# Reordering the tail of a fused hash-attention and mixture-of-adapters kernel: the gates, the sums and tile 5

## The chip, the cores and the metric

The kernel runs on one core of a Trainium2 chip. The metric is the device time of one execution in microseconds. A core has five engines with one instruction queue each: TensorE (PE) for matmuls, VectorE (DVE), ScalarE (ACT), GpSimd (POOL), and SyncE (SP), which here issues most of the transfers. An engine takes its instructions in the order in which the program gives them, so the order in which Python emits work is the order on each engine.

## The reference

Two stages. First an attention over 4 batches, 8 heads, 768 positions and 64 columns, in which a query sees only the keys of its own hash bucket (6 sign bits of a projection). The heads of a position, side by side, give a row x of 512 numbers, 3072 rows in all. Then a mixture of 8 low-rank adapters adds a correction to each row:

```
logits = x @ w_gate                      # 8 numbers a row
topk = the two largest logits            # K = 2
w = exp(sel - max) / sum                 # weights of the two
delta = sum over the two of w * ((x @ A[e]) @ B[e])     # rank 16
out = x + delta
```

## The kernel before, in words

Rows are handled in tiles of 128; a batch has six of them, numbered 0 to 5. The attention runs over 16 pairs of heads (four to a batch); each pair has six slots of scores, whose exponentials ACT takes. The adapter work of a batch is spread over the slots of the next one, except for the last batch, which has nothing behind it: its adapter work is the tail of the kernel, and the change is made there.

The tail is written out by hand, in `lasts` (from slot 2 of the last pair) and in `end`. It splits the six tiles into three groups: H is tiles 0, 1 and 2, I is tiles 3 and 4, J is tile 5. A group goes through these steps:

- `normt` (L360 to L380): DVE divides the attention sums by their denominators; for J it writes a bf16 copy for the transpose, and `xf` (L382) has ACT write the fp32 values of tile 5 into x, in two instructions.
- `turnt` (L390): PE transposes the last 128 columns, ACT or DVE copies them back.
- `lgz` (L402): PE multiplies by the gate weights and all A matrices side by side: 8 logits and 128 numbers z a row, in a PSUM tile lz (lzH, lzI, lzJ).
- the gates. For H, `route1` and `route_exp` leave a mask m and exponentials e; `gates` (L431) then has DVE make gw (L436) and zm = z times gw (L438), and `gsum` (L444) the sum and its reciprocal rt. For I and J, `top` (L453) has DVE find the two largest logits and ACT take the exponentials (L462); `gates1` (L465) then has DVE make gw with its sum (L474), zm and rt. For one tile alone (J) `gates1` multiplies zm by rt at once (L480); for two tiles rt is kept for later (L483, L484).
- `zt` (L493): PE transposes zm (L500), ACT copies the result to zT (L502).
- `product` (L504): PE multiplies zT by all B matrices into a 128x512 PSUM tile d (d0 to d5).
- `total` (L518): out = d times rt plus x. DVE does it in one instruction (L526); with `split`, ACT multiplies (L523) and POOL adds x (L524).
- `store` (L528): one tile of 256 KB goes to the output, from SP's queue or from ACT's.

In the kernel before, `end` orders this so: gates of H follow `normt` of J and `xf`; the sums of tiles 0 (split), 1 (DVE) and 2 (split) follow; then `gates1` of I, `zt` of I, `gates1` of J, `zt` of J, then products 3, 4 and 5. Tile 5 is summed on PE: two fp32 matmuls with the identity (L959) put x of tile 5 into d5, the product is added to it, and ACT copies d5 out (L972). The stores stand in SP's queue in the order of tiles 1, 0, 3, 2, 4; that of tile 5 is on ACT's queue.

Of the kernel before, what the change touches and what calls it, by code (L numbers as in the profile page):

```python
# [12 lines left out]
F32 = mybir.dt.float32  # L13
BF16 = mybir.dt.bfloat16
AX = mybir.AxisListType
ALU = mybir.AluOpType
# [3 lines left out]
class Emitter:  # L20
# [407 lines left out]
        self.nc.scalar.activation(out=e, in_=d, func=ACT.Exp)  # L428
        self.rg[b, I] = (m, e)

    def gates(self, b, I):  # L431
        nc, P, E, r, n = self.nc, self.P, self.E, self.r, len(I)
        lz = self.lz[b, I]
        m, e = self.rg[b, I]
        gw = self.smallp.tile([P, n, E], F32, tag=f"gw{n}", name=f"gw{b}_{I[0]}")
        nc.vector.tensor_mul(out=gw, in0=m, in1=e)  # L436
        zm = self.zm[b, I] = self.smallp.tile([P, n, self.ER], BF16, tag=f"zm{n}", name=f"zm{b}_{I[0]}")
        nc.vector.tensor_tensor(  # L438
            out=zm.rearrange("p n (e r) -> p n e r", e=E),
            in0=lz[:, :, E:].rearrange("p n (e r) -> p n e r", e=E),  # L440
            in1=gw.unsqueeze(3).to_broadcast([P, n, E, r]), op=ALU.mult)
        self.rg[b, I] = gw

    def gsum(self, b, I):  # L444
        nc, P, n = self.nc, self.P, len(I)
# [19 lines left out]
    def gates1(self, b, I):  # L465
        nc, P, E, r, n = self.nc, self.P, self.E, self.r, len(I)
        lz = self.lz[b, I]
        top, e = self.rg[b, I]
        gw = self.smallp.tile([P, n, E], F32, tag=f"gw{n}", name=f"gw{b}_{I[0]}")
        ss = self.smallp.tile([P, n], F32, tag=f"ss{n}", name=f"ss{b}_{I[0]}")  # L470
        zm = self.zm[b, I] = self.smallp.tile([P, n, self.ER], BF16, tag=f"zm{n}", name=f"zm{b}_{I[0]}")
        rt = self.smallp.tile([P, n], F32, tag=f"rt{n}", name=f"rt{b}_{I[0]}")
        for i in range(n):
            nc.vector.scalar_tensor_tensor(out=gw[:, i], in0=lz[:, i, 0:E], scalar=top[:, i, 1:2], in1=e[:, i],  # L474
                                           op0=ALU.is_ge, op1=ALU.mult, accum_out=ss[:, i:i + 1])
        z4, l4 = zm.rearrange("p n (e r) -> p n e r", e=E), lz[:, :, E:].rearrange("p n (e r) -> p n e r", e=E)
        g4 = gw.unsqueeze(3).to_broadcast([P, n, E, r])
        if n == 1:
            nc.vector.reciprocal(out=rt, in_=ss)
            nc.vector.scalar_tensor_tensor(out=z4[:, 0], in0=l4[:, 0], scalar=rt, in1=g4[:, 0],  # L480
                                           op0=ALU.mult, op1=ALU.mult)
            return
        nc.vector.tensor_tensor(out=z4, in0=l4, in1=g4, op=ALU.mult)  # L483
        nc.vector.reciprocal(out=rt, in_=ss)  # L484
        for j, i in enumerate(I):
            self.rt[b, i] = rt[:, j:j + 1]
# [428 lines left out]
    def end(self):  # L915
        nc, P, b, Z = self.nc, self.P, self.B - 1, self.LZ
        H, I, J = (0, 1, 2), (3, 4), (5,)
        self.s_ctx.close()
        pe = self.tc_ctx.enter_context(self.tc.tile_pool(name="ps_e", bufs=1, space=bass.MemoryType.PSUM, reuse_waits="tile"))

        def bank(t):
            return lambda shape, dt, name: pe.tile(shape, dt, tag=t, name=name)

        x0, x1, x2, y0, y1, y2 = (bank(t) for t in ("x0", "x1", "x2", "y0", "y1", "y2"))
        f = [P, 512]
        lz = lambda a, n: a[:, 0:n * Z].rearrange("p (n z) -> p n z", n=n)
        self.pvt(I, 4)
        self.unit(J, x0(f, F32, "pvJ"))
        lzI = lz(x1(f, F32, "lzI"), 2)
        for i in I:  # L930
            self.lgz(b, I, i, range(3), lzI)
        self.normt(I, True)
        self.route_exp(b, H)
        self.pvt(J, 5)
        self.normt(J)
        self.turnt(I, x2, nc.scalar.copy)
        lzJ = lz(y1(f, F32, "lzJ"), 1)
        self.lgz(b, J, 5, range(3), lzJ)
        self.turnt(J, y0, nc.scalar.copy)
        self.xf(J)  # L940
        self.gates(b, H)
        for i in I:
            self.lgz(b, I, i, (3,))
        self.lgz(b, J, 5, (3,))
        self.zt(b, H, y2)
        self.top(b, I)
        self.top(b, J)
        self.gsum(b, H)
        d0, d1, d2 = self.m(f, F32, "d0"), x2(f, F32, "d1"), self.vt(f, F32, "d2")
        self.product(b, 0, d0)  # L950
        self.product(b, 1, d1)
        self.total(b, 0, d0, True)
        self.total(b, 1, d1)
        self.store(b, 0, 1)
        self.store(b, 0, 0)
        self.product(b, 2, d2)
        self.total(b, 2, d2, True)
        d5 = x0(f, F32, "d5")
        nc.tensor.matmul(out=d5, lhsT=self.ident, rhs=self.x[b][:, 5, :], start=True, stop=False,  # L959
                         skip_group_check=True)  # L960
        self.gates1(b, I)
        self.zt(b, I, y2)
        self.gates1(b, J)
        d3, d4 = y0(f, F32, "d3"), x1(f, F32, "d4")
        self.zt(b, J, self.m)
        self.product(b, 3, d3)
        self.product(b, 4, d4)
        self.total(b, 3, d3)
        self.store(b, 1, 1)
        self.store(b, 1, 0)  # L970
        self.product(b, 5, d5, False)
        nc.scalar.copy(out=self.out_to(b, 5), in_=d5)  # L972
        self.total(b, 4, d4)
        self.store(b, 2, 0)
        self.store(b, 2, 1, nc.scalar)


# [46 lines left out]
```

## Time and profile before

| | |
|---|---|
| three runs | 162.53, 163.56, 164.48 us |
| median | 163.56 us |
| the profiled execution, its time | 162.41 us |
| its span, first to last instruction | 160.6 us |
| busy share of the span | PE 93%, ACT 90%, POOL 69%, DVE 68% |
| mean granted TensorE clock | 0.994 |

All times in views of the trace count from the start of the span, which is 1.8 us shorter than the time of its execution. In a timeline row the first number is the start, the second the time from the start of the first to the end of the last of the merged instructions, then engine, line, operation, what is written and read, shapes and count; what stands in brackets is idle time of that engine just ahead and the instruction that ended it. An instruction can start before the one ahead of it on its engine has ended where it does not need its result.

### The profile page before, as it was taken

What the parts mean: (1) busy time and instruction counts of PE and PEld (TensorE: products, weight loads), DVE (VectorE), ACT (ScalarE), POOL (GpSimd) and SP (SyncE); (2) the same over time, 40 slices, a digit from 0 to 9 for tenths busy, and PEclk for the clock granted to TensorE, in tenths of its full rate; (3) what the DMA queues carried; (4) which work ended last, traced back from release to release, by engine and by line L of the source; (5) the groups of instructions that cost most, each with busy time, mean ns of one, the idle gap of its engine ahead of it and who ended that gap; (6) DMA issues with size and microseconds to landing.
All of it is one profiled execution on the core that took longest, in us unless ns stands there. A gap on an engine that the chain in (4) does not pass through costs nothing.

```text
span 160.6 us, 5335 instructions
## 1 busy us (share of the span) xinstructions
PE 148.6 (93%) x2172; PEld 100.8 (63%) x2172; DVE 109.1 (68%) x291; ACT 144.2 (90%) x126; POOL 111.5 (69%) x166
## 2 busy tenths in 40 slices
PE   6898999999999999999998999999999999999730
PEld 2345676676767676667755676667666766788300
DVE  5798895746464976778556976687677527666760
ACT  3798889999999999999997999999999999998830
POOL 7866999998979786969199767988498825320140
PEclk9999999999999999999999999999999999999997
DMA  5996559899998986989979997999788920854054
GB/s 142 291 373 187 172 159 180 230 247 206 260 218 166 267 164 148 232 196 356 169 231 246 291 252 180 253 267 339 162 173 217 230 58 18 234 172 147 2 205 187
DMA packets 57594, 33.03 MB, mean 206 GB/s; under 512 B 42978, under 2 KB 55266, under 8 KB 57570
## 3 DMA queue, kind: packets, MB, share of 16 engines
q1 hardware_dynamic: 57296, 32.43, 80.1%
q8 instruction: 17, 0.28, 0.7%
q10 hardware_dynamic: 274, 0.27, 0.5%
q14 instruction: 7, 0.06, 0.1%
HBM read 20.16 MB, written 7.03 MB: 169 GB/s over the span
## 4 chain that ended last, share of the span: by engine, by line
PE 82%; DVE 8%; DMA 3%; issue 1%; DVEq 1%; ACT 0%; SPq 0%
PE s L283 36%; PE pv L303 19%; PE hs L193 7%; PE pv L291 4%; PE tr L241 4%; DMA nat<-in_k_dram 3%; PE lz L407 3%; PE dl L505 2%; PE warm L646 2%; DVE aug L570 1%; DVE R L180 1%; DVE aug L589 1%; DVE acc L526 1%; DVE x L323 1%; DVEq L1019 1%
## 5 line engine op out<-in xcount | busy, mean ns | idle before, releaser
L286 ACT ACTIVATE P<-s 128x1536 bf16<-128x1536 f32 x96 | 133.9, 1451 | 4.5 <-PE s L283 3.1
L283 PE MATMUL s<-aug 71*128 71x512 bf16 (+2 forms) x432 | 78.5, 308 | 0.9 <-DVE aug L570 0.7
L283 PEld LDWEIGHTS <-aug 71*128 71x128 bf16 x432 | 34.6, 97 | 21.6 <-issue 5.8
L303 PEld LDWEIGHTS <-P 128*128 128x128 bf16 x1080 | 42.1, 98 | 8.2
L303 PE MATMUL pv<-vb,P 128*128 128x65 bf16 x1080 | 44.3, 193 | 0.0
L261 POOL COPY aug<-aug 64x768 bf16<-64x768 bf16 x30 | 24.8, 827 | 14.8 <-DMA aug<-nb 12.3
L180 DVE STREAM_TRANSPOSE R<-nat 128x384 f32<-128x384 f32 x62 | 33.2, 559 | 2.1 <-DMA nat<-in_k_dram 1.9
L232 POOL CAST nb<-nat 128x768 bf16<-128x768 f32 x30 | 24.6, 823 | 2.1 <-DMA nat<-in_k_dram 1.2
L333 POOL CAST xb<-x 128x768 bf16<-128x768 f32 x15 | 12.3, 823 | 12.3 <-DVE x L323 5.8
L526 DVE SCALAR_TENSOR_TENSOR acc<-dl,rt,x 128x512 f32<-128x512 f32 x18 | 13.5, 748 | 7.9 <-PE dl L505 7.9
L323 DVE TENSOR_TENSOR x<-pv,ri 128x384 f32<-128x384 f32 x30 | 16.7, 557 | 1.0
L170 POOL TENSOR_TENSOR vs<-vn 128x384 f32<-128x384 f32 x16 | 15.9, 994 | 0.0
L321 DVE RECIPROCAL ri<-pv 128x6 f32<-128x6 f32 x30 | 5.8, 195 | 14.7 <-PE pv L303 14.6
L247 DVE TENSOR_SCALAR aug<-tr 128x768 bf16<-128x768 bf16 x20 | 11.0, 550 | 5.7 <-PE tr L241 2.3
L193 PE MATMUL hs<-R,hst 128*32 128x192 f32 x240 | 14.0, 332 | 0.0
L168 POOL CAST vb<-vn 128x768 bf16<-128x768 f32 x16 | 13.2, 826 | 0.2 <-DMA vn<-in_v_dram 0.2
L193 PEld LDWEIGHTS hs<-R,hst 128*32 128x32 f32 x240 | 6.7, 109 | 6.3 <-DVE ri L321 4.1
L291 PE MATMUL pv<-vb,eps 128*128 128x390 bf16 x30 | 10.1, 337 | 0.6 <-DVE gw L436 0.3
L241 PE MATMUL tr<-ident_bf,nb 128*128 128x128 bf16 x120 | 10.0, 219 | 0.0
L524 POOL TENSOR_TENSOR acc<-acc,x 128x512 f32<-128x512 f32 x2 | 2.5, 1268 | 9.3 <-ACT acc L523 9.3
L173 POOL TENSOR_TENSOR vb<-vs,vs 128x128 bf16<-128x128 f32 x16 | 7.3, 456 | 1.3
L172 POOL TENSOR_TENSOR vs<-vs 128x128 f32<-128x128 f32 x16 | 7.3, 454 | 1.3
(115 smaller groups left out, 112.3 us busy)
## 6 DMA issues: line engine op xcount, KB each, us to landing
vn<-in_v_dram SPq DMA_DIRECT2D x16, 384.0 KB, 8.1
nat<-in_q_dram SPq DMA_DIRECT2D x15, 384.0 KB
nat<-in_k_dram SPq DMA_DIRECT2D x15, 384.0 KB, 3.9
out_dram<-acc SPq DMA_DIRECT2D x7, 512.0 KB, 4.3
out_dram<-acc SPq DMA_DIRECT2D x9, 256.0 KB, 3.4
dr<-sg SPq DMA_DIRECT2D x14, 48.0 KB, 2.5
aug<-dr SPq DMA_DIRECT2D x14, 48.0 KB
nat<-in_q_dram SPq DMA_DIRECT2D x2, 192.0 KB
```

Of the source, the lines that this page charges most:

```text
L170: nc.gpsimd.tensor_add(out=s3, in0=vn[:, :, 0:3, :], in1=vn[:, :, 3:6, :])
L180: self.nc.vector.transpose(out=self.R[p][:, i, h, :], in_=self.nat[p][:, i, h, :])
L193: nc.tensor.matmul(out=hs[32 * j:32 * j + 32], lhsT=self.hst[:, hf].rearrange("p b i -> p (b i)"), rhs=rhs, start=(hf == 0), stop=(hf == 1 ...
L232: self.nc.gpsimd.tensor_copy(out=self.nb[p][:, i].rearrange("p t h d -> p h t d"), in_=self.nat[p][:, i].rearrange("p h (t d) -> p h t d", ...
L241: self.nc.tensor.transpose(out=tr[:, t, :], in_=self.nb[p][:, i, t].rearrange("p h d -> p (h d)"), identity=self.ident_bf)
L261: self.nc.gpsimd.tensor_copy(out=a[0:64, :, 2 + i, :], in_=a[64:128, :, i, :])
L283: nc.tensor.matmul(out=ps[:, o:o + w].rearrange("p (t c) -> p t c", c=P), lhsT=aug[0:71, kt, 2 * h + 1, :], rhs=rhs, start=True, stop=True)
L286: nc.scalar.activation(out=self.P_[p][:, s * W:end], in_=ps, func=ACT.Exp, scale=128.0)
L291: self.nc.tensor.matmul(out=pv, lhsT=self.eps, rhs=self.vb[p % 3][:, h, T:T + 1, :].to_broadcast([self.P, T, D + 1]), start=True, stop=Fal ...
L303: self.nc.tensor.matmul(out=pv[:, i, :], lhsT=self.P_[p][:, o:o + P], rhs=vb[:, h, kt, :], start=False, stop=(kt == T - 1), skip_group_che ...
L323: nc.vector.tensor_tensor(out=self.x[b][:, :, c:c + D], in0=pv[:, :, 0:D], in1=ri.unsqueeze(2).to_broadcast([P, T, D]), op=ALU.mult)
L526: nc.vector.scalar_tensor_tensor(out=out, in0=ps, scalar=rt, in1=self.x[b][:, i, :], op0=ALU.mult, op1=ALU.add)
```

## The change

The gates of H are split: `gates` makes gw ahead of `normt` of J, and the new `gated` makes zm right after it. `xf` moves from behind `turnt` of J to a place behind the sums of tiles 0 to 2. `zt` of H moves ahead of the last `lgz` step of J. `gates1` of I moves ahead of the sum of tile 1, and `zt` of I ahead of the split sum of tile 2. Product 2 moves ahead of the sum of tile 0. Products 3 and 4 move ahead of `zt` of J. The identity matmuls and ACT's copy of tile 5 go; DVE sums tile 5 with `total`, and for that `gates1` no longer has a form of its own for one tile. The order of the stores in the queues stays as it was.

```diff
--- before.py
+++ after.py
@@ -428,18 +428,24 @@
         self.nc.scalar.activation(out=e, in_=d, func=ACT.Exp)
         self.rg[b, I] = (m, e)
 
-    def gates(self, b, I):
+    def gates(self, b, I, then=True):
         nc, P, E, r, n = self.nc, self.P, self.E, self.r, len(I)
         lz = self.lz[b, I]
         m, e = self.rg[b, I]
         gw = self.smallp.tile([P, n, E], F32, tag=f"gw{n}", name=f"gw{b}_{I[0]}")
         nc.vector.tensor_mul(out=gw, in0=m, in1=e)
+        self.rg[b, I] = gw
+        if then:
+            self.gated(b, I)
+
+    def gated(self, b, I):
+        nc, P, E, r, n = self.nc, self.P, self.E, self.r, len(I)
+        lz, gw = self.lz[b, I], self.rg[b, I]
         zm = self.zm[b, I] = self.smallp.tile([P, n, self.ER], BF16, tag=f"zm{n}", name=f"zm{b}_{I[0]}")
         nc.vector.tensor_tensor(
             out=zm.rearrange("p n (e r) -> p n e r", e=E),
             in0=lz[:, :, E:].rearrange("p n (e r) -> p n e r", e=E),
             in1=gw.unsqueeze(3).to_broadcast([P, n, E, r]), op=ALU.mult)
-        self.rg[b, I] = gw
 
     def gsum(self, b, I):
         nc, P, n = self.nc, self.P, len(I)
@@ -475,11 +481,6 @@
                                            op0=ALU.is_ge, op1=ALU.mult, accum_out=ss[:, i:i + 1])
         z4, l4 = zm.rearrange("p n (e r) -> p n e r", e=E), lz[:, :, E:].rearrange("p n (e r) -> p n e r", e=E)
         g4 = gw.unsqueeze(3).to_broadcast([P, n, E, r])
-        if n == 1:
-            nc.vector.reciprocal(out=rt, in_=ss)
-            nc.vector.scalar_tensor_tensor(out=z4[:, 0], in0=l4[:, 0], scalar=rt, in1=g4[:, 0],
-                                           op0=ALU.mult, op1=ALU.mult)
-            return
         nc.vector.tensor_tensor(out=z4, in0=l4, in1=g4, op=ALU.mult)
         nc.vector.reciprocal(out=rt, in_=ss)
         for j, i in enumerate(I):
@@ -931,47 +932,45 @@
             self.lgz(b, I, i, range(3), lzI)
         self.normt(I, True)
         self.route_exp(b, H)
+        self.gates(b, H, False)
         self.pvt(J, 5)
         self.normt(J)
+        self.gated(b, H)
         self.turnt(I, x2, nc.scalar.copy)
         lzJ = lz(y1(f, F32, "lzJ"), 1)
         self.lgz(b, J, 5, range(3), lzJ)
         self.turnt(J, y0, nc.scalar.copy)
-        self.xf(J)
-        self.gates(b, H)
         for i in I:
             self.lgz(b, I, i, (3,))
+        self.zt(b, H, y2)
         self.lgz(b, J, 5, (3,))
-        self.zt(b, H, y2)
         self.top(b, I)
         self.top(b, J)
         self.gsum(b, H)
         d0, d1, d2 = self.m(f, F32, "d0"), x2(f, F32, "d1"), self.vt(f, F32, "d2")
         self.product(b, 0, d0)
         self.product(b, 1, d1)
+        self.product(b, 2, d2)
         self.total(b, 0, d0, True)
+        self.gates1(b, I)
         self.total(b, 1, d1)
         self.store(b, 0, 1)
         self.store(b, 0, 0)
-        self.product(b, 2, d2)
+        self.zt(b, I, y2)
         self.total(b, 2, d2, True)
-        d5 = x0(f, F32, "d5")
-        nc.tensor.matmul(out=d5, lhsT=self.ident, rhs=self.x[b][:, 5, :], start=True, stop=False,
-                         skip_group_check=True)
-        self.gates1(b, I)
-        self.zt(b, I, y2)
+        self.xf(J)
         self.gates1(b, J)
-        d3, d4 = y0(f, F32, "d3"), x1(f, F32, "d4")
-        self.zt(b, J, self.m)
+        d3, d4, d5 = y0(f, F32, "d3"), x1(f, F32, "d4"), x0(f, F32, "d5")
         self.product(b, 3, d3)
         self.product(b, 4, d4)
+        self.zt(b, J, self.m)
         self.total(b, 3, d3)
         self.store(b, 1, 1)
         self.store(b, 1, 0)
-        self.product(b, 5, d5, False)
-        nc.scalar.copy(out=self.out_to(b, 5), in_=d5)
+        self.product(b, 5, d5)
         self.total(b, 4, d4)
         self.store(b, 2, 0)
+        self.total(b, 5, d5)
         self.store(b, 2, 1, nc.scalar)
 
 
```

## The prediction

> **What bounds the kernel now.** I read the page's head first, then the chain of work that ended last, then the timeline of each engine from 147 us on, and last the transfers in short windows. Most of the 160.6 us lies ahead of the change and is the same program in both kernels; only what comes after 148.5 us can move.
>
> ```profile
> span 160.6 us, 5335 instructions
> ```
>
> The chain of work, cut to the tail, says who sets the order there:
>
> ```profile
> 151.39 0.75 DVE acc L526
> 152.14 0.30 DVE gw L474 x4
> ...
> 154.44 1.18 DVEq L1019
> ```
>
> DVE's sum of tile 1 (L526) is followed by the gates of tiles 3 and 4 on the same engine: these waited for the sum, not for their data. The chain then ends at DVE's queue at 155.62, five microseconds before the span does. What fills these five is seen in the stores (SP's rows one by one, ACT's row, SP's waits at the end) and in the DMA share by window (last two columns: share, GB/s):
>
> ```profile
> 152.17 0.33 SPq L535 DMA_DIRECT2D out_dram<-acc  x1
> 153.23 0.33 SPq L535 DMA_DIRECT2D out_dram<-acc  x1
> 154.99 0.33 SPq L535 DMA_DIRECT2D out_dram<-acc  x1
> 155.42 0.38 SPq L535 DMA_DIRECT2D out_dram<-acc  x1
> 155.89 0.41 SPq L535 DMA_DIRECT2D out_dram<-acc  x1
> ...
> 155.36 0.38 ACTq L535 DMA_DIRECT2D out_dram<-acc  x1
> ...
> L1019 SPq EVENT_SEMAPHORE  x7: 17/28/28, 159.1 to 160.6; - x7
> ```
> ```profile
> 153.00:153.75 0.75, 0.25 (x3) 0.08 (x4) 0.60 (x4) 0.37 (x1) 0.75 (x2) 1.00 0.92 350
> ...
> 154.05:154.80 0.75, 0.66 (x3) 0.10 (x1) 0.59 (x1) 0.27 (x2) 0.38 (x1) 1.00 0.91 347
> 154.80:155.75 0.95, 0.00 (x0) 0.00 (x0) 0.82 (x2) 0.53 (x1) 0.00 (x0) 1.00 0.01 2
> 156.00:158.50 2.50, 0.00 (x0) 0.00 (x0) 0.00 (x0) 0.00 (x0) 0.00 (x0) 1.00 1.00 380
> 158.50:158.75 0.25, 0.00 (x0) 0.00 (x0) 0.00 (x0) 0.00 (x0) 0.00 (x0) 0.70 0.37 131
> ```
>
> Six stores of 262144 bytes. A store issued at 152.17 has its first bytes at 153.00, so 0.83 after the issue begins. The first two go alone. Then the DMA engines idle for 0.95, and four stores, issued within 0.9 us, queue at a share of 1.00 until about 158.59 (158.50 plus 0.37 of 0.25). At 380 GB/s one store takes 0.69; at the 350 of a lone one 0.75. So the end is a queue of transfers; the engines set only when each store joins it. From the last byte to the span's end lie 2.0 us of landing and closing that I leave as they are.
>
> **The change part by part.** The rows of the trace before that carry the terms, DVE, then ACT, then PE and POOL:
>
> ```profile
> 148.80 0.29 DVE L372 TENSOR_TENSOR xbt<-pvJ,rit 128x128 bf16<-128x128 f32 x1
> 149.01 0.17 DVE L436 TENSOR_TENSOR gw<-m,e 128x24 f32<-128x24 f32 x1
> 149.22 0.56 DVE L438 TENSOR_TENSOR zm<-lzH,gw 128x384 bf16<-128x384 f32 x1
> 149.73 0.25 DVE L457 MAX8 top<-lzI 128x8 f32<-128x8 f32 x2
> ...
> 150.56 0.18 DVE L449 RECIPROCAL rt<-ss 128x3 f32<-128x3 f32 x1
> 152.06 0.22 DVE L474 SCALAR_TENSOR_TENSOR gw<-lzI,top,e 128x8 f32<-128x8 f32 x1
> 152.46 0.42 DVE L483 TENSOR_TENSOR zm<-lzI,gw 128x256 bf16<-128x256 f32 x1
> 152.80 0.15 DVE L484 RECIPROCAL rt<-ss 128x2 f32<-128x2 f32 x1
> 152.88 0.20 DVE L474 SCALAR_TENSOR_TENSOR gw<-lzJ,top,e 128x8 f32<-128x8 f32 x1
> 153.32 0.35 DVE L480 SCALAR_TENSOR_TENSOR zm<-lzJ,rt,gw 128x128 bf16<-128x128 f32 x1
> 154.21 1.41 DVE L526 SCALAR_TENSOR_TENSOR acc<-d,rt,x 128x512 f32<-128x512 f32 x2 [0.54 <-PE d L505]
> ```
> ```profile
> 149.58 0.52 ACT L388 ACTIVATE x<-pvJ,rit 128x64 f32<-128x64 f32 x2
> 150.21 0.48 ACT L502 COPY zT<-ztp 128x384 bf16<-128x384 bf16 x1
> 150.59 0.43 ACT L462 ACTIVATE e<-lzI,nt 128x8 f32<-128x8 f32 x2
> ...
> 151.17 1.26 ACT L523 ACTIVATE acc<-d,rt 128x512 f32<-128x512 f32 x2
> 153.27 0.37 ACT L502 COPY zT<-ztp 128x256 bf16<-128x256 bf16 x1 [0.83 <-PE ztp L500]
> 154.00 0.27 ACT L502 COPY zT<-ztp 128x128 bf16<-128x128 bf16 x1 [0.36 <-PE ztp L500]
> 154.74 0.58 ACT L972 COPY acc<-d 128x512 f32<-128x512 f32 x1 [0.48 <-PE d L505]
> ```
> ```profile
> 149.84 0.34 PE L500 MATMUL ztp<-ident_bf,zm 128*128 128x128 bf16 x3
> 150.75 0.82 PE L505 MATMUL d<-Bcat,zT 128*128 128x512 bf16 x3 [0.57 <-ACT zT L502]
> 151.40 1.02 PE L959 MATMUL d<-x,ident 128*128 128x512 f32 x2
> 152.94 0.28 PE L500 MATMUL ztp<-ident_bf,zm 128*128 128x128 bf16 x2 [0.52 <-DVE zm L483]
> ...
> 151.94 2.49 POOL L524 TENSOR_TENSOR acc<-acc,x 128x512 f32<-128x512 f32 x2 [9.31 <-ACT acc L523]
> ```
>
> *Split gates of H, `xf` later.* gw of H drops into the time in which DVE waited for PE ahead of tile 5's reciprocal, so it costs nothing there; without that gap it would cost the 0.2 from gw to zm in the rows. zm moves from 149.22 to 149.01, the transposes from 149.84 to 149.63, their copy on ACT from 150.21 to 150.00. `xf` ended at 150.10 and would have held that copy, so its move gives about half of the 0.21. The exponentials of I go from 150.59 to 150.38 and end 0.43 later, at 150.81; the maxima at 149.73 hang on PE's logits and stay, and so does rt of H at 150.56. The last logit step of J now stands behind the transposes on PE, a delay under 0.1 that DVE's two maxima of I cover; what waits for it, J's exponential, has a microsecond to spare.
>
> *Gates of I ahead of the sum of tile 1.* gw starts at 150.85 instead of 152.06; from there by the rows to zm 0.40 and to its end 0.42, so 151.67. The sum of tile 1 takes its place behind the reciprocal, 0.08 after it: 151.67 to 152.42, where it ended at 152.14. This is the price: the first store goes from 152.17 to 152.45.
>
> *`zt` of I and the split sums.* Transposes 0.06 after zm, 151.73 to 152.01; PE is free, because the 1.02 us of identity matmuls are gone. Tile 0's part on ACT goes from 151.17 to 150.97 and ends at 151.65, so the copy to zT (372 ns) runs from 152.05 to 152.42, 1.2 earlier than before. Tile 2's part on ACT now stands behind that copy: 152.33 to 153.01, 0.57 later than before. POOL covers this: its first sum ends at about 153.0, its second runs from 153.1 to 154.36 (it ended at 154.43). Without that cover tile 2's store would come 0.57 later.
>
> *Products 3 and 4, gates of J, `xf`.* Product 3 at 152.48, done at 152.87. On DVE gw of J at 152.34 (two sums in a row start 0.66 apart, from 1.41 less 0.75), zm about 0.25 later (bounds 0.20, half of I's 0.40, and 0.44, from gw to zm in the old form with the reciprocal between), 0.29 long like the 128-wide row at 148.80: 152.87. Sum 3 from 152.91, sum 4 from 153.57, sum 5 from 154.23 to 154.98. Sum 5 needs d5: transpose 152.93 to 153.16, ACT's `xf` ends near 153.45, then the copy (0.27), the product (0.39 and 0.06 of wait): 154.16. That margin is thin, but a delay there moves only the last store. In place of ACT's copy (0.58) DVE does one more sum (0.75), and the old end of sums, 155.62, becomes 154.98.
>
> *The stores*, as issued before and after: tile 1 152.17, 152.45; tile 0 153.23, 153.02; tile 3 154.99, 153.68; tile 2 155.42, 154.39; tile 4 155.89, 154.87 (0.48 behind the issue ahead of it, as now); tile 5, on ACT, 155.36, 155.02. Adding 0.83, they join the queue at 153.28, 153.85, 154.51, 155.22, 155.70 and 155.85. With 0.69 each the DMA engines end them at 153.97, 154.66, 155.35, 156.04, 156.73 and 157.42: none finds the queue empty, and the idle 0.95 of the window rows is gone. 158.59 less 157.42 is 1.17; with 0.75 each the end is 157.78 and the gain 0.81. I take 0.69, since back to back is how they now run, and call it 1.2. The bound on the other side is the last store alone, issued at 155.02: 155.85 plus 0.75 is 156.60, a gain of 2.0.
>
> [...]
>
> Sum: 162.41 less 1.2 is 161.2 for the profiled execution. That execution lies 1.15 under the median of the runs shown, so the forecast for a median is 163.56 less 1.2, 162.4.
>
> **The rivals.** *R1, the queue is faster than thought:* the end is set by the last store alone, gain 2.0, 161.6. For it: the first bytes of lone stores reach 0.9 share at once. Against: 380 GB/s at a share of 1.00 leaves nothing.
>
> [...]
>
> *R4, the change does not do what it says:* the exponentials of I stay late, at 150.59, since ACT is held by something else. Then gates, first store and all else come 0.21 later, a gain near 1.0; that lies inside the forecast's own range.
>
> **How the numbers follow.** The forecast (R4 in it) 0.62, R1 0.13, R2 0.12, R3 0.08, something not seen 0.05. The forecast's own gain is 0.8 to 1.4; the runs shown spread by 1 us about their median, and a median of few runs by about 0.7. 1% is 1.6 us, about what a measurement of this kernel can tell from no change. The forecast reaches over it by spread in 4 of 10 cases (0.25), R1 mostly (0.11): faster 0.36. R3 and the unseen pass 1% on the slow side in 0.06; the rest, 0.58, is within. Range: 161.0, R1 less half a microsecond of spread, to 163.9, R2 with a little; R3 is left out.
>
> **What would show it.** Right: a first store near 152.45 and a third near 153.7; zm of I ending near 151.7 and zm of J near 152.9; three sums in a row on DVE ending near 155.0; no idle DMA window from 153.3 on, and the last bytes near 157.4; a span near 159.4. Wrong: sums of over 0.8 us or POOL sums over 1.3 where they overlap (R2, R3); a last sum that waits for ACT beyond 155.6; gaps in the DMA share between stores; a first store after 153.

## The result, and the profile after

| | before | changed |
|---|---|---|
| median of 20 runs each | 163.72 us | 162.0 us |
| the profiled execution, its span | 162.41, 160.6 us | 162.86, 161.1 us |
| ratio of times | | 0.9918, 95% interval 0.9891 to 0.9945 |

The kernel became faster by 0.82%, 1.34 us (0.9 to 1.8 by the interval). The ratio is of the runs in the faster of two states alone, so it is not that of the two medians, which lie 1.72 us apart. The forecast was 1.2 us less and a median of 162.4.

The profiled execution after has a *longer* span than the one before, so spans cannot be compared as they are. Its last score exponential on ACT, which ends the part that both kernels share, ended later (first row: the kernel before, six of them merged; second row: the changed kernel):

```profile
139.39 8.38 ACT L286 ACTIVATE P<-s 128x1536 bf16<-128x1536 f32 x6 [0.33 <-PE s L283]
```
```profile
span 161.1 us, 5327 instructions
...
147.98 1.45 ACT L286 ACTIVATE P<-s 128x1536 bf16<-128x1536 f32 x1
```

It ended at 147.77 before and at 149.43 after, 1.66 later; nothing ahead of it was changed. From here on, times with a plus count from that end. So counted, the tail to the end of the span took 12.86 before and 11.64 after: 1.2 less. The tail repeats far better than the kernel: the same program profiled a second time gave 11.64 again (e1 and e10 below show the one exception).

The stores of the changed kernel, tiles 1, 0, 3, 2, 4 from SP's queue and tile 5 from ACT's, and the DMA windows (a row has its length, the busy time of PE, of PE's weight loads, of DVE, ACT and POOL, then the granted clock, the DMA share and GB/s; the share reads up to 1.01 here):

```profile
154.07 0.33 SPq L536 DMA_DIRECT2D out_dram<-acc  x1
154.67 0.33 SPq L536 DMA_DIRECT2D out_dram<-acc  x1
155.34 0.33 SPq L536 DMA_DIRECT2D out_dram<-acc  x1
156.03 0.33 SPq L536 DMA_DIRECT2D out_dram<-acc  x1
156.46 0.41 SPq L536 DMA_DIRECT2D out_dram<-acc  x1
...
156.66 0.36 ACTq L536 DMA_DIRECT2D out_dram<-acc  x1
```
```profile
154.07:154.90 0.83, 0.67 (x3) 0.21 (x3) 0.80 (x5) 0.83 (x4) 0.73 (x2) 1.00 0.00 0
154.90:155.00 0.10, 0.00 (x0) 0.00 (x0) 0.10 (x1) 0.10 (x2) 0.10 (x1) 1.00 0.90 348
155.00:159.00 4.00, 0.39 (x1) 0.10 (x1) 1.63 (x3) 0.23 (x2) 1.01 (x1) 0.77 1.01 380
159.00:159.25 0.25, 0.00 (x0) 0.00 (x0) 0.00 (x0) 0.00 (x0) 0.00 (x0) 0.50 0.23 74
```

The two idle stretches of the kernel before are gone. From 154.9, 0.83 after the first issue, the DMA engines run at a share of 1.01 and 380 GB/s for the whole four microseconds, and 1.9 us after the queue runs dry the span ends, as before. Read to 0.01 us from the last packet of the stores, the last byte was written at +10.95 before (158.72) and +9.75 after (159.18). That number is used below; the window rows bracket it.

The engine rows behind the stores, DVE, ACT and POOL of the changed kernel:

```profile
150.66 0.55 DVE L445 TENSOR_TENSOR zm<-lzH,gw 128x384 bf16<-128x384 f32 x1
...
152.48 0.23 DVE L480 SCALAR_TENSOR_TENSOR gw<-lzI,top,e 128x8 f32<-128x8 f32 x1
...
152.90 0.42 DVE L484 TENSOR_TENSOR zm<-lzI,gw 128x256 bf16<-128x256 f32 x1
...
153.31 0.73 DVE L527 SCALAR_TENSOR_TENSOR acc<-d,rt,x 128x512 f32<-128x512 f32 x1
...
154.56 2.07 DVE L527 SCALAR_TENSOR_TENSOR acc<-d,rt,x 128x512 f32<-128x512 f32 x3
```
```profile
151.65 0.48 ACT L503 COPY zT<-ztp 128x384 bf16<-128x384 bf16 x1 [0.31 <-PE ztp L501]
152.02 0.43 ACT L468 ACTIVATE e<-lzI,nt 128x8 f32<-128x8 f32 x2
```
```profile
153.37 2.63 POOL L525 TENSOR_TENSOR acc<-acc,x 128x512 f32<-128x512 f32 x2 [9.09 <-ACT acc L524]
```

The exponentials of tiles 3 and 4 (152.02) end at 152.45, and the gates that need them (152.48) now stand ahead of the sum of tile 1 (153.31), and the last three sums follow one another without a gap, the last ending at 156.63.

### The profile page after: what moved, and what is told of

The parts are those of the page before. It is cut to its first block, busy times and chain, and to the rows that moved or that the text cites. A ratio compares the mean times of both kernels' runs of the same rounds, so it can differ in the third digit from the quotient of the medians.

```text
span 161.1 us, 5327 instructions
## 1 busy us (share of the span) xinstructions
PE 148.5 (92%) x2169; PEld 101.0 (63%) x2170; DVE 108.9 (68%) x292; ACT 143.0 (89%) x125; POOL 111.6 (69%) x166
## 4 chain that ended last, share of the span: by engine, by line
PE 67%; DVE 11%; DMA 10%; POOL 5%; issue 2%; ACT 1%; DVEq 0%; SPq 0%; POOLq 0%
PE s L283 28%; PE pv L303 16%; DMA nat<-in_k_dram 6%; PE hs L193 6%; DMA aug<-nb 3%; PE tr L241 3%; PE pv L291 3%; PE dl L506 2%; DVE R L180 2%; PE lz L407 2%; PE warm L647 2%; POOL nb L232 1%; DVE aug L571 1%; DVE x L323 1%; DVE aug L590 1%
## 5 line engine op out<-in xcount | busy, mean ns | idle before, releaser
L525 POOL TENSOR_TENSOR acc<-acc,x 128x512 f32<-128x512 f32 x2 | 2.5, 1266 | 9.2 <-ACT acc L524 9.1
L241 PEld LDWEIGHTS <-nb 128*128 128x128 bf16 x120 | 7.3, 97 | 1.9 <-POOL vb L173 1.0
```

Source lines behind the costliest of these rows:

```text
L241: self.nc.tensor.transpose(out=tr[:, t, :], in_=self.nb[p][:, i, t].rearrange("p h d -> p (h d)"), identity=self.ident_bf)
```

## The experiments

Two theories were set against each other. The *queue theory* is the prediction's: the last byte is set by a queue of 256 KB transfers that takes 0.69 us for each, and an engine matters only through the moment at which its store joins. *Rival W:* the end follows the last piece of engine work, which also came earlier (from 155.62 before to 156.63 less 1.66, 154.97, after). A second rival, *P*, gives the gain to the 1.0 us of identity matmuls that PE no longer runs. All kernels were profiled; most were timed too, against the kernel before on the same chip. Times alone cannot tell most of them apart (the intervals are 0.4 to 0.6% to either side), the tails can. In the profiled executions of e1, e5 and e6 the granted clock fell to a half for 3.41 us at 87 to 92 us, far ahead of the tail (mean granted clock 0.972, 0.975 and 0.981; more in the last section); each of the three programs was therefore profiled once more, as e10, e11 and e9. The second profiles do not show that fall (means 0.976, 0.985 and 0.992), and their spans are 2.8, 1.5 and 5.1 us shorter.

**e0, the changed kernel again.**

> The changed kernel once more, to see how far the tail repeats from one profile to the next. Both theories: last byte at 9.75 us from the end of the last score exponential, within 0.1; the time within 0.3% of the changed kernel's.

Last byte at +9.75, the same to 0.01; ratio 0.9923 (0.9881 to 0.9965), against 0.9918. Differences of 0.1 us in a tail can be trusted where nothing else differs, the granted clock included.

**e4, a late last sum.** The edit, ahead of `total(b, 5, d5)`:

```diff
+        junk = self.singles.tile([P, 512], F32, name="junk")
+        nc.vector.scalar_tensor_tensor(out=junk, in0=d4, scalar=self.rt[b, 4], in1=self.x[b][:, 4, :],
+                                       op0=ALU.mult, op1=ALU.add)
         self.total(b, 5, d5)
```

> The changed kernel with one more DVE instruction of the form of a sum (0.66 us from start to start) ahead of the sum of tile 5; its result is used by nothing. Queue theory: the last store has 0.88 us of slack in the queue, so the last byte stays at 9.75 from the end of the last score exponential and the time is that of the changed kernel. Rival W: 0.66 later, 10.41.

The extra instruction, the last sum, and the last store with the windows in which the queue ran dry:

```profile
147.73 1.45 ACT L286 ACTIVATE P<-s 128x1536 bf16<-128x1536 f32 x1
...
157.06 0.35 ACTq L536 DMA_DIRECT2D out_dram<-acc  x1
```
```profile
155.63 0.74 DVE L974 SCALAR_TENSOR_TENSOR junk<-d,rt,x 128x512 f32<-128x512 f32 x1
156.29 0.74 DVE L527 SCALAR_TENSOR_TENSOR acc<-d,rt,x 128x512 f32<-128x512 f32 x1
```
```profile
158.50:158.75 0.25, 0.00 (x0) 0.00 (x0) 0.00 (x0) 0.00 (x0) 0.00 (x0) 0.50 1.00 385
158.75:159.00 0.25, 0.00 (x0) 0.00 (x0) 0.00 (x0) 0.00 (x0) 0.00 (x0) 0.50 0.16 49
```

The last store was issued at +7.88 (157.06 less 149.18) instead of +7.23, and the last byte came at +9.74. The last engine work has at least 0.65 us to spare: W falls. The time, a ratio of 0.997 (0.9934 to 1.0005), lies above what the tail says, though its interval reaches close to it; the tail is the finer measure.

**e5 and e11, a later last sum.** The edit is that of e4 with two of the instruction.

> The changed kernel with two more DVE instructions of the form of a sum (1.32 us) ahead of the sum of tile 5; their result is used by nothing. Queue theory: the last store's slack of 0.88 is used up and the rest shows: last byte 0.4 later, 10.15 from the end of the last score exponential. Rival W: 1.32 later, 11.07.

> The same kernel as e5_later_last_sum, the changed kernel with two more DVE instructions ahead of the sum of tile 5, for a profile at a higher granted clock. By the rule that the runs so far fit, the last store, issued near 8.68, ends alone at 8.68 + 0.97 + 0.69 = 10.34. Rival W: 11.07.

Ratio 0.9986 (0.9946 to 1.0026). Last byte at +10.35 in e5 and +10.36 in e11, the last issue at +8.68 and +8.67. The rows are of e11; the window's share of 0.58 shows the queue run empty before the last store:

```profile
158.50 0.35 ACTq L536 DMA_DIRECT2D out_dram<-acc  x1
```
```profile
158.25:159.75 1.50, 0.00 (x0) 0.00 (x0) 0.21 (x1) 0.00 (x0) 0.00 (x0) 0.50 0.58 221
```

So there is a kink, as a queue has one: the first 0.65 us cost nothing, the next 0.79 cost 0.6. The first expectation was 0.2 too low: it took two instructions as 1.32 where the issue moved by 1.45, and the tail of a lone store as 1.55 where it is 1.67.

**e6 and e9, one more transfer.** The edit:

```diff
         self.store(b, 0, 1)
+        more = self.scr.tile([P, 512], F32, tag="more", name="more")
+        nc.sync.dma_start(out=more, in_=self.acc[b, 0][:, 1])
         self.store(b, 0, 0)
```

> The changed kernel with one more transfer of 256 KB in SP's queue, behind the store of tile 1: the same data once more, to a scratch tensor in memory. No engine does more. Queue theory: a seventh store in a queue that never empties costs 0.69, last byte at 10.44 from the end of the last score exponential, and the time is 0.7 us above that of the changed kernel. Rival W: the last store is on ACT's queue and its issue does not move, so 9.75, at most 10.1 by SP's issue time of 0.33.

> The same kernel as e6_extra_store, the changed kernel with one more transfer of 256 KB, for a profile at a higher granted clock. Queue theory: last byte at 10.44 from the end of the last score exponential. Rival W: 9.75 to 10.1.

Ratio 0.9979 (0.994 to 1.0017), between the changed kernel and the one before. Last byte at +10.46 (e6) and +10.44 (e9), while the last store was issued at +7.23 as ever. Rows of e9:

```profile
146.93 1.45 ACT L286 ACTIVATE P<-s 128x1536 bf16<-128x1536 f32 x1
...
155.60 0.35 ACTq L536 DMA_DIRECT2D out_dram<-acc  x1
```
```profile
153.90:158.50 4.60, 0.39 (x1) 0.10 (x1) 1.67 (x3) 0.27 (x2) 1.05 (x1) 0.96 1.01 382
158.50:158.75 0.25, 0.00 (x0) 0.00 (x0) 0.00 (x0) 0.00 (x0) 0.00 (x0) 0.50 0.71 254
```

A transfer that no engine waits for costs 0.69 to 0.71, the price of one place in the queue. With it the last byte comes from SP's queue; ACT's store ended 0.3 earlier.

**e1 and e10, tile 5 on DVE alone**, in the kernel before:

```diff
         d5 = x0(f, F32, "d5")
-        nc.tensor.matmul(out=d5, lhsT=self.ident, rhs=self.x[b][:, 5, :], start=True, stop=False,
-                         skip_group_check=True)
...
-        self.product(b, 5, d5, False)
-        nc.scalar.copy(out=self.out_to(b, 5), in_=d5)
+        self.product(b, 5, d5)
         self.total(b, 4, d4)
         self.store(b, 2, 0)
+        self.total(b, 5, d5)
```
(and `gates1` without its form for one tile)

> The kernel before with one part of the change: tile 5 summed by DVE, without the identity matmuls on PE and without ACT's copy. Counted from the end of the last score exponential, the last byte was written at 10.95 us in the kernel before and at 9.75 in the changed one. Queue theory (the end is a queue of six stores): sum 3 comes 0.1 earlier because zm of tile 5 no longer waits for its reciprocal, so the last byte is at 10.85, and the time is that of before within 0.2 us. Rival W (the end follows the last piece of engine work): three sums in a row on DVE end 0.3 later than the last sum did, so 11.3. Rival P (the gain comes from the 1.0 us of PE freed of identity matmuls): 10.0 or less.

> The same kernel as e1_tile5_alone, the kernel before with tile 5 summed by DVE alone, for a profile at a higher granted clock. Queue theory: last byte at 10.85 from the end of the last score exponential. Rival W: 11.3. Rival P: 10.0 or less.

Ratio 1.0026 (0.998 to 1.0073). In e1 the last byte came at +10.84 although the last store was issued at +8.44, 0.3 later than in the kernel before: neither W (+11.3) nor P (+10.0). In e10, the same program, it came at +11.14. The third store tells why, +7.12 in e1 and +7.42 in e10, and ahead of it the three products on PE (first row e1, the others e10; the first busy time in a window is that of PE's matmuls, the third number from the end the granted clock, here 1.00 and 0.50):

```profile
158.95 0.82 PE L500 MATMUL d<-Bcat,zT 128*128 128x512 bf16 x3
```
```profile
155.93 1.46 PE L500 MATMUL d<-Bcat,zT 128*128 128x512 bf16 x3
```
```profile
151.75:155.16 3.41, 1.42 (x10) 0.54 (x9) 2.62 (x16) 2.74 (x9) 1.06 (x1) 1.00 0.01 2
155.16:157.00 1.84, 1.66 (x6) 0.43 (x6) 0.87 (x5) 0.64 (x2) 1.42 (x2) 0.50 0.75 285
```

At 155.16 the granted clock fell to a half, the products took 1.46 us instead of 0.82, and the third store and the whole queue behind it came 0.3 later. So this part of the change alone gained 0.1 us in one execution and lost 0.2 in the other: the identity matmuls by themselves were not the gain. P falls. What their absence is worth together with the early gates can be read from e2.

**e2, the gates alone**, in the kernel before:

```diff
         self.product(b, 1, d1)
+        self.product(b, 2, d2)
         self.total(b, 0, d0, True)
+        self.gates1(b, I)
         self.total(b, 1, d1)
...
-        self.product(b, 2, d2)
-        self.total(b, 2, d2, True)
         d5 = x0(f, F32, "d5")
...
-        self.gates1(b, I)
         self.zt(b, I, y2)
+        self.total(b, 2, d2, True)
```

> The kernel before with the other part of the change: product 2 and the gates of tiles 3 and 4 ahead of the sum of tile 1, their transposes ahead of the split sum of tile 2; the identity matmuls stay, ahead of these transposes on PE. Last byte counted from the end of the last score exponential (10.95 before, 9.75 changed). Queue theory: the identity matmuls hold the transposes back by 0.7, the third store is issued near 6.6 where the changed kernel has 5.9, and the last byte is at 10.25, half of the gain. Rival W: the last issue comes 0.4 earlier than before, so 10.55. Rival P: no gain, 10.95.

Ratio 0.9935 (0.9876 to 0.9994); last byte at +10.61, not +10.25. The queue held; the time of the third store was forecast wrong: +6.88 instead of 6.6, where the changed kernel has +5.91. The rows tell where the 0.97 between the two kernels lies (the last exponential; DVE; ACT; PE; the third store):

```profile
147.93 1.45 ACT L286 ACTIVATE P<-s 128x1536 bf16<-128x1536 f32 x1
```
```profile
153.07 0.42 DVE L483 TENSOR_TENSOR zm<-lzI,gw 128x256 bf16<-128x256 f32 x1
```
```profile
154.18 0.37 ACT L502 COPY zT<-ztp 128x256 bf16<-128x256 bf16 x1 [0.71 <-PE ztp L500]
```
```profile
153.01 1.02 PE L959 MATMUL d<-x,ident 128*128 128x512 f32 x2
153.86 0.28 PE L500 MATMUL ztp<-ident_bf,zm 128*128 128x128 bf16 x2
154.99 0.23 PE L500 MATMUL ztp<-ident_bf,zm 128*128 128x128 bf16 x1 [0.85 <-DVE zm L480]
155.06 0.91 PE L505 MATMUL d<-Bcat,zT 128*128 128x512 bf16 x3
```
```profile
156.26 0.33 SPq L535 DMA_DIRECT2D out_dram<-acc  x1
```

- Late gates of tiles 0 to 2, which this kernel still has: zm of tiles 3 and 4 ends at +4.12, 0.22 later than in the changed kernel, and the first store goes out at +4.86 instead of +4.64. The expectation left this out.
- Identity matmuls: zm ended at 153.49, the transposes start at 153.86. In the changed kernel they start 0.06 behind zm, so the identity matmuls hold them back by 0.31, not by the 0.7 of the expectation.
- Order of the products: those of tiles 3 and 4 stand behind the transpose of tile 5 on PE's queue here, as in the kernel before. Their input, ACT's copy, ended at 154.55; they start at 155.06, where the changed kernel has 0.06 between the two. That is 0.45, which the expectation left out too.

The three add up to 0.98. So removing the identity matmuls and moving the products are worth something once the gates are early; this is read from one trace, not from runs with each alone. From the measured third store the queue gives +10.61, and that is what was seen. W would give nearly the same number here, so this run does not tell the two apart.

**e3, the gates back**, in the changed kernel:

```diff
         self.total(b, 0, d0, True)
-        self.gates1(b, I)
         self.total(b, 1, d1)
         self.store(b, 0, 1)
         self.store(b, 0, 0)
-        self.zt(b, I, y2)
         self.total(b, 2, d2, True)
+        self.gates1(b, I)
+        self.zt(b, I, y2)
```

> The changed kernel with the gates of tiles 3 and 4 put back behind the sum of tile 1, and their transposes behind the split sum of tile 2. Queue theory: the first store is issued 0.5 earlier, the third 1.0 later (near 6.9 from the end of the last score exponential), the queue runs empty between them, and four stores from there end at 10.55; 0.4 of the gain of 1.2 is left. Rival W: the last sum ends near 8.2, 0.3 later than in the kernel before, so 11.05. Rival P (freed PE time is the gain): 9.75.

Ratio 0.9972 (0.993 to 1.0014); last byte at +10.63. The last exponential and the third store:

```profile
148.33 1.44 ACT L286 ACTIVATE P<-s 128x1536 bf16<-128x1536 f32 x1
...
156.68 0.33 SPq L536 DMA_DIRECT2D out_dram<-acc  x1
```

The first store went out 0.47 earlier (+4.17), the third 1.0 later (+6.91), and the end with the third. The move of the gates is worth 0.9 of the 1.2 us, but only together with the rest: e2 has it without the rest and gains 0.34.

**e7, the split undone**, in the changed kernel:

```diff
-        self.gates(b, H, False)
         self.pvt(J, 5)
         self.normt(J)
-        self.gated(b, H)
...
         self.turnt(J, y0, nc.scalar.copy)
+        self.xf(J)
+        self.gates(b, H)
...
         self.total(b, 2, d2, True)
-        self.xf(J)
```

> The changed kernel with the gates of tiles 0 to 2 whole and behind the norm of tile 5 again, and ACT's fp32 values of tile 5 back in their early place. The term of the prediction: zm of tiles 0 to 2, its copy on ACT, the exponentials and the gates behind it all come 0.21 later, so all stores do: last byte 0.2 later, 9.95 from the end of the last score exponential. If this step is off the path: 9.75.

Ratio 0.9954 (0.9914 to 0.9995); last byte at +9.97, all six stores 0.22 to 0.23 later than in the changed kernel. The term was 0.21. The last exponential and the first store:

```profile
148.80 1.44 ACT L286 ACTIVATE P<-s 128x1536 bf16<-128x1536 f32 x1
...
155.11 0.33 SPq L536 DMA_DIRECT2D out_dram<-acc  x1
```

**e8, the gates of tiles 0 to 2 whole and early**, in the changed kernel:

```diff
-        self.gates(b, H, False)
+        self.gates(b, H)
         self.pvt(J, 5)
         self.normt(J)
-        self.gated(b, H)
+        self.gsum(b, H)
...
-        self.turnt(J, y0, nc.scalar.copy)
+        self.zt(b, H, y2)
         for i in I:
             self.lgz(b, I, i, (3,))
-        self.zt(b, H, y2)
-        self.lgz(b, J, 5, (3,))
-        self.top(b, I)
-        self.top(b, J)
-        self.gsum(b, H)
+        self.turnt(J, y0, nc.scalar.copy)
...
         self.product(b, 0, d0)
+        self.lgz(b, J, 5, (3,))
         self.product(b, 1, d1)
         self.product(b, 2, d2)
+        self.top(b, I)
         self.total(b, 0, d0, True)
+        self.top(b, J)
         self.gates1(b, I)
```

> The changed kernel with the gates of tiles 0 to 2 whole ahead of the norm of tile 5, their transposes and products ahead of the last logit steps and of tile 5's, and ACT's part of the sum of tile 0 ahead of tile 5's exponential. The rule that the runs so far fit: last byte = issue of a store + 0.97 + 0.69 for it and each store behind it, whichever store gives the most. In the changed kernel the stores of tiles 1, 0, 3 and 2 give 9.75, 9.66, 9.64 and 9.65 from the end of the last score exponential, so only a shift of all four helps. By the rows the exponentials of tiles 3 and 4 no longer wait for a copy on ACT and start 0.1 to 0.2 earlier, the gates and the stores of tiles 1, 3 and 2 0.1, that of tile 0 0.3: last byte 9.64, 0.1 us less, which the time cannot show. If the norm of tile 5 behind the gates holds something back: above 9.75.

Ratio 0.9921 (0.9877 to 0.9964), last byte at +9.76: no gain. The exponentials of tiles 3 and 4 did come 0.16 earlier (+2.44 against +2.59), but DVE stood still ahead of the gates:

```profile
151.44 0.17 DVE L463 MAX8 top<-lzJ 128x8 f32<-128x8 f32 x1 [0.40 <-PE lzJ L407]
151.64 0.15 DVE L465 TENSOR_SCALAR nt<-top 128x1 f32<-128x1 f32 x1
151.71 0.22 DVE L480 SCALAR_TENSOR_TENSOR gw<-lzI,top,e 128x8 f32<-128x8 f32 x1
```

The maximum of tile 5 stands ahead of them in DVE's queue and waited 0.40 for logits that the later norm of tile 5 had put off (its bf16 copy starts at +1.46 here, at +1.03 in the changed kernel). The gates start at +3.08, against +3.06. No version was found that beats the changed kernel.

**One rule for all runs.** With n the number of stores from one on to the last, the last byte is the issue of that store + 0.97 + 0.69 n, for whichever store gives the most:

| kernel | deciding store | issued at | n | by the rule | measured |
|---|---|---|---|---|---|
| before | tile 3 | +7.22 | 4 | 10.95 | 10.95 |
| changed; e0; e4 | tile 1 | +4.64 | 6 | 9.75 | 9.75; 9.75; 9.74 |
| e1; e10 | tile 3 | +7.12; +7.42 | 4 | 10.85; 11.15 | 10.84; 11.14 |
| e2 | tile 3 | +6.88 | 4 | 10.61 | 10.61 |
| e3 | tile 3 | +6.91 | 4 | 10.64 | 10.63 |
| e5; e11 | tile 5 | +8.68; +8.67 | 1 | 10.34; 10.33 | 10.35; 10.36 |
| e6; e9 | tile 1 | +4.65; +4.64 | 7 | 10.45; 10.44 | 10.46; 10.44 |
| e7 | tile 1 | +4.86 | 6 | 9.97 | 9.97 |
| e8 | tile 1 | +4.66 | 6 | 9.77 | 9.76 |

The two constants were read off the first two rows (10.95 less 7.22 is 3.73 for four stores, 9.75 less 4.64 is 5.11 for six); the others follow to within 0.03, in queues of one to seven. For e8 and e11 the rule was written down ahead of the run; what it does not give is the issue of a store, which e2 and e8 show to be the harder part to forecast.

## Why the prediction was right

Taken against the same zero, the steps that carry the forecast came within 0.07 us of it. In the kernel before's time (the rows after, less 1.66): zm of tiles 0 to 2 forecast at 149.01, measured 149.00; its copy on ACT 150.00, 149.99; exponentials of tiles 3 and 4 150.38, 150.36; their gates 150.85, 150.82; end of zm 151.67, 151.66; end of the last sum 154.98, 154.97. The six stores: forecast 152.45, 153.02, 153.68, 154.39, 154.87 and 155.02, measured 152.41, 153.01, 153.68, 154.37, 154.80 and 155.00. The product of tile 5 was done at 154.02 instead of 154.16, which left the thin margin ahead of the last sum 0.14 wider.

Part of the closeness is luck. The last byte came at 157.52, not at 157.42, and the kernel before's at 158.72, not at the 158.59 that was read from the window rows. By the rule above a queue takes 0.14 on top of the 0.83 and 0.69 a store; the forecast left these 0.14 out for the changed kernel, and its reading for the kernel before was early by about as much, so the difference of the two was not touched.

- *What bounds the tail.* Right: a queue of transfers. e4, e5 and e6 show it: late engine work that costs nothing until the slack is gone, and an idle engine's extra transfer that costs its full place.
- *The size.* Forecast 1.2, measured 1.20 in the tails and 1.34 (0.9 to 1.8) in the times. The measured 0.82% is the case that the forecast gave 0.58, a change of under 1%. The median of 162.0 is 0.4 below the forecast one; the tails have no such 0.4, so it is taken as spread of the runs. The term of 0.69 for a store held, in the changed kernel and in e6. The lower bound by 0.75 for a store took the time of a lone one for each place; in the rule the excess is paid once, in the 0.97. The 380 GB/s behind the 0.69 stand in the window after again.
- *The price.* The first store is 0.24 later (+4.40 to +4.64), forecast 0.28. e3 shows the trade: without it the first store is earlier and the end 0.9 later.
- *R1, the last store alone.* Wrong: its issue moved by 0.65 in e4 with no effect.
- *R2 (chance 0.12) and R3 (0.08), sums of DVE and POOL that would wait for one another where they overlap,* put the time at 163.7 and 164.3, and R2 gave the range its upper end. Wrong: this was the author's supposition, and no run shows such a wait. In the kernel before, the sum that starts at 154.21 already overlaps POOL's second sum, which ends at 154.43, and no sum there takes over 751 ns. In the changed kernel both directions can be read. POOL's first sum began at 153.37, while the sum of tile 1, ahead by 0.06, ran on DVE (153.31 to 154.04): POOL did not wait for DVE. The sum of tile 4 began at 155.23, in the middle of POOL's second (154.74 to 156.01): DVE did not wait for POOL. The rows of the sums, DVE and POOL before, then DVE and POOL after, are

```profile
L526 DVE SCALAR_TENSOR_TENSOR acc<-d,rt,x x3: 743/750/751, 151.4 to 154.9; 128x512 f32<-128x512 f32 x3
...
L524 POOL TENSOR_TENSOR acc<-acc,x x2: 1267/1268/1269, 151.9 to 153.2; 128x512 f32<-128x512 f32 x2
```
```profile
L527 DVE SCALAR_TENSOR_TENSOR acc<-d,rt,x x4: 731/740/751, 153.3 to 155.9; 128x512 f32<-128x512 f32 x4
```
```profile
L525 POOL TENSOR_TENSOR acc<-acc,x 128x512 f32<-128x512 f32 x2 | 2.5, 1266 | 9.2 <-ACT acc L524 9.1
```

so the sums of DVE take 731 to 751 ns (743 to 751 before) and those of POOL 1266 on average (1268 before). POOL's two ended 2.63 after the first began, 2.49 before, because the second now waits for ACT's part of tile 2, which ends at 154.66.
- *R4, exponentials that stay late.* Did not happen; e7 shows what it would have cost, 0.22.
- *What was left open.* That moving `xf` gives half of the 0.21 was not tried apart from the split, nor the move of products 3 and 4 or the identity matmuls inside the changed kernel. Which part is worth how much has no single answer: the gates alone give 0.34 (e2), tile 5 on DVE alone 0.1 or a loss (e1, e10), taking the gates out of the whole loses 0.9 (e3).
- *What the prediction did not see* is a rival that could have cost it 0.3: in e10, without the identity matmuls, PE's granted clock fell to a half at 155.16, ahead of the last three products (below). In the seven profiles of the changed kernel and of its variants with the same order ahead of the last sum (e0, e4, e5, e6, e9, e11), the clock fell at +5.78 or later, when the products that the first five stores need were done (154.74 in the changed kernel, +5.31). Whether it falls earlier in other executions is open.

## What to carry to other kernels

Where a kernel ends in stores, write down for each its issue and the number of stores from it to the last; the largest of issue + a constant (0.97 us here) + that number times the time of one (0.69 here) was the end in all 14 profiles, to within 0.03, and the work worth moving is that ahead of the deciding store, even at the price of a later first one. An average share of DMA hides this: look for empty windows between stores. To compare tails, count from the last event that both kernels share, not from the start of the span.

## What the runs showed of the hardware that was not expected

PE's granted clock can fall to a half while PE still has work, as in e10. The 14 profiles show 17 falls: one in each tail, and one at 87 to 88 us in e1, e5 and e6. Those in the tails stand at another place in each execution: +10.82 in the kernel before, +7.74 in the changed one and +9.8 in e0, the same program, +5.23 in e10, +5.8 in e4, +9.74 in e9. Counted back from a fall in stretches of 3.41 us, the length of the falls in the middle, those with 1.05 us of matmuls (changed kernel, 153.76 to 157.17), 1.42 (e10) and 1.56 (e4, 151.56 to 154.97) ended in a fall, and so did the one without any in e9 (154.71 to 158.12) and in the kernel before; those with 1.92 (the kernel before), 1.99 (e9, 151.30 to 154.71) and 2.16 (changed kernel, 150.34 to 153.76) did not. The rows of e10 above show 1.42 us of matmuls in 151.75 to 155.16 and the half clock behind it. In the kernel before, the last stretch with matmuls held most of those on the identity too, 1.92 us in all, and the clock stayed at full through the next stretch, with its idle PE, to 158.59:

```profile
151.77:155.18 3.41, 1.92 (x8) 0.38 (x6) 2.77 (x13) 1.74 (x5) 2.49 (x2) 1.00 0.41 154
155.18:158.59 3.41, 0.00 (x0) 0.00 (x0) 0.44 (x1) 0.15 (x1) 0.00 (x0) 1.00 0.80 306
158.59:160.60 2.01, 0.00 (x0) 0.00 (x0) 0.00 (x0) 0.00 (x0) 0.00 (x0) 0.50 0.01 3
```

In e10 a stretch that was 42% busy (1.42 of 3.41) was followed by a fall. The cost was 0.3 us in e10, through three products that took 1.46 us instead of 0.82.

More time went with a fall in the middle. The page of e1 has the granted clock in 40 slices of 4.1 us, in tenths:

```profile
PEclk9999999999999999999996999999999999999985
```

The one slice at 6 tenths is that from 87.0 to 91.2 us. The last score exponential ended at 153.04 in e1 and at 149.93 in e10, the same program, 3.1 us earlier, and the span of e1 is 2.8 us longer, more than twice what the change gains. That the busy share is what decides, and that the half clock is the whole of the 2.8 us, was not tested by itself; both are read from where the falls stood.
